# Square sums with a fifth group on GpSimd, rows added before their column sums, and a first fold in quarters

## The chip, the core and the metric

The kernel runs on one core of one Trainium2 chip. The metric is the device time of one execution in microseconds (us), taken as the median of several runs. TensorE does the matrix products (PE in the rows below, PEld for its weight loads), VectorE is DVE, ScalarE is ACT, GpSimd is POOL, and SyncE (SP) issues nearly all DMAs. SBUF is the on-chip memory, PSUM the memory into which TensorE adds up.

## What is computed

Attention over channels, then two feed-forward layers, all in float32 from outside. Cut to what matters:

```python
qn = q / (np.linalg.norm(q, axis=1, keepdims=True) + 1e-06)    # q, k, v: 6016 x 256
kn = k / (np.linalg.norm(k, axis=1, keepdims=True) + 1e-06)
s = kn.transpose(0, 2, 1) @ qn / tau                           # 256 x 256
s = s - s.max(-1, keepdims=True)
a = np.exp(s)
a /= a.sum(-1, keepdims=True) + 1e-09
x = v @ a
h = x @ moe_w_in;  x = (h * np.cos(h)) @ moe_w_out             # 2048 hidden
h = x @ moe2_w_in; x = (h / (1 + np.exp(-h))) @ moe2_w_out
```

The change touches the norms (sums of squares over all 6016 tokens), the softmax, and the place where the softmax is multiplied into the first layer's weights.

## The kernel before

**Loading and scores.** q and k come in 25 groups, two chunks of 128 tokens each but for three groups of one. For each group SP issues a load (L529) into one of seven buffers, TensorE multiplies k by q (L619, two halves of k, `a` = 0 and 1, into `S[0]` and `S[1]`), and ScalarE squares the group (L651). The squares are added up on VectorE into `acc` (L668), except for the groups in `SIDE`, which GpSimd adds into `aside` (L663); one square buffer (`SQ_BUFS`) serves GpSimd's groups, two PSUM buffers serve VectorE's. At group `JOINED` the two sums are added (L670). In the groups named in `FINE` TensorE uses split operands (L608).

**Held-back scores.** For the last `LATE` groups only half `a` = 0 is multiplied in the loop. The other half is kept back as filler for TensorE: some of it behind the column sums, the rest behind the matmul that spreads the norms.

**Norm chain.** TensorE sums `acc` over its 128 partitions with eight one-column products (L677: two rows of 512, four columns blocks each), then one for tau (L678). Then: square root on ScalarE (L683), plus 1e-6 and reciprocal on VectorE (L684, L685), a diagonal matrix `aside` with the norms (L686 on ScalarE, L687 on VectorE), tau (L690, L691), a matmul that spreads the diagonal over all rows (L693), a copy (L696).

**Softmax and fold.** For each half `a`: scaling (L701), maximum (L704), exponential (L705), two transposes on TensorE (L712), a copy to `ET` (L713). The first fold multiplies `ET` into the first 512 columns of the first layer's weights (L761), in halves of 256 columns; ScalarE and VectorE scale the result to a high part (L769) and a low part (L773) in `wa`. Layer one begins after it (L856). The remaining folds (`f1` to `f3`, L743) follow between units of layer one.

**Weights.** The weights come as 64-bit words: a load (`l` for the output weights, `lW` for the input weights, L279), then `a..`/`b..`/`d..` begin with the absolute value on ScalarE (L345) and a rounding of the low word (L297 on ScalarE, L299 on GpSimd), `c..` clamp and shift on VectorE (L304, L312), `j..` join on VectorE and GpSimd (L318, L321), `s..` split on ScalarE and GpSimd (L369, L370). The last letter is W for input and O for output weights. `s0`, `v0`, `s1`, `v1` split the first two blocks of v on ScalarE (L504) and GpSimd (L507).

**Order.** The schedule is written by hand: each engine runs its instructions in the order in which the program emits them, and strings such as `FRONT`, `AFTER`, `BEFORE` and `EARLY` say at which point a step is emitted. A unit `i` of layer one is: products h (L856), sine on ScalarE (L1215), product with the cosine on VectorE (L1218), high part (L867, ScalarE) and low part (L871, VectorE) of the unit before, and the output products of the unit two before (L884).

Of the kernel before, what the change touches and what calls it, by code (L numbers as in the profile page):

```python
# [20 lines left out]
P = 128  # L21
C = 256
# [24 lines left out]
ASIDE = [("wo2", 5), ("wo2", 6), ("wo2", 7)]  # L47
GROUPS = [1, 1] + 22 * [2] + [1]
FIRST = 2
LATE = 4  # L50
REST = 2
TAU = 9
SQ_BUFS = 1
FINE = {5: 'v', 8: 'v', 10: 'v', 13: 'a'}
BEHIND = 3
WARM = (9, 0)
# [11 lines left out]
EARLY = {  # L68
# [3 lines left out]
    'outer': {  # L72
        0: 'x1 l', 1: 'aO', 2: 'p1 cO lW', 3: 'e1 l10 l11 p2 w10 w11', 4: 'l', 5: 'dO', 6: 'rO cO',
        7: 'e2 l20 l21 w20 w21', 9: 'aO', 10: 'cO', 11: 'e3 l30 l31 w30 w31',
    },
}
# [151 lines left out]
def direct(ctx, tc, qk, vT, tau, w_in1, w_out1, w_in2, w_out2, outT, dp, kept, within):  # L228
# [302 lines left out]
    for eng in (nc.sync, nc.scalar, nc.sync):  # L531
# [66 lines left out]

    fine = {}

    def emit_scores(g, both=range(CH)):
        c0 = sum(GROUPS[:g])
        if g in fine:
            kinds = fine[g]
            for j in range(GROUPS[g]):
                for a in both:
                    for i, k in PASSES:
                        nc.tensor.matmul(  # L608
                            S[a],
                            kinds[i][:, j, 1, a * P : (a + 1) * P],  # L610
                            kinds[k][:, j, 0, :],
                            start=False,
                            stop=False,
                            skip_group_check=True,
                        )
            return
        for j in range(GROUPS[g]):
            for a in both:
                nc.tensor.matmul(  # L619
                    S[a],  # L620
                    tiles[g][:, j, 1, a * P : (a + 1) * P],
                    tiles[g][:, j, 0, :],
                    start=(c0 + j == 0),
                    stop=(c0 + j == NCK - 1),
                    skip_group_check=True,
                )

    for g, n in enumerate(GROUPS):
        c0 = sum(GROUPS[:g])
        if g == len(tiles):  # L630
            load_group(nc.sync)
        t = tiles[g]
        if g == 0:
            nc.vector.memset(ones, 1.0)
            nc.vector.memset(rtau, 0.0)
            nc.vector.memset(sums, 1e-9)
            make_identity(nc, ident)
            warm_up(N[:, :P], WARM[0])
# [12 lines left out]
        nc.scalar.activation(sq[:, :n], t[:, :n].rearrange("p g s d -> p g (s d)"), AF.Square)  # L651
        if g in FINE:
            k = len(fine)
            hi, lo = [w[k // 2][:, k % 2].rearrange("p j (s c) -> p j s c", s=2) for w in (wa, wo1)]
            fine[g] = (hi, lo)
            if FINE[g] == "a":
                nc.scalar.activation(hi, t, AF.Copy)
            else:
                nc.vector.tensor_scalar(out=hi, in0=t, scalar1=1.0, scalar2=1.0, op0=ALU.mult, op1=ALU.mult)
            nc.gpsimd.tensor_tensor(out=lo, in0=t, in1=hi.bitcast(F32), op=ALU.subtract)  # L660
        if g in SIDE:
            if g > SIDE[0]:
                nc.gpsimd.tensor_tensor(out=aside, in0=aside, in1=sq, op=ALU.add)  # L663
        elif c0 < GMAX:
            assert c0 + n <= GMAX
            nc.vector.tensor_copy(acc[:, c0 : c0 + n], sq[:, :n])
        else:
            nc.vector.tensor_tensor(out=acc[:, :n], in0=acc[:, :n], in1=sq[:, :n], op=ALU.add)  # L668
        if g == JOINED:
            nc.vector.tensor_tensor(out=acc, in0=acc, in1=aside, op=ALU.add)  # L670
        steps_of(FRONT.get(g, ""))
    steps_of(AFTER)

    for j in range(GMAX - 1, -1, -1):
# [3 lines left out]
    nc.tensor.matmul(N[:, 2 * CH : 2 * CH + 1], ones, rtau, start=False, stop=True, skip_group_check=True)  # L678
    steps_of(THEN[0])
    late = range(len(GROUPS) - LATE, len(GROUPS))  # L680
    for g in late[:REST]:
        emit_scores(g, (1,))
    nc.scalar.activation(r.rearrange("p s a -> p (s a)"), N[:, : 2 * CH], AF.Sqrt)  # L683
    nc.vector.tensor_scalar_add(r, r, 1e-6)  # L684
# [71 lines left out]
    def fold_half(m):  # L756
        fold_room(0, m)
        for a in range(CH):
            pws[0, a] = pws[0, a][:, : TB // 2]
            for d in range(CH):  # L760
                nc.tensor.matmul(  # L761
                    pws[0, a],
                    ET[:, d, a * P : (a + 1) * P],
                    w1[:, d, m * TB // 2 : (m + 1) * TB // 2],
                    start=(d == 0),
                    stop=(d == CH - 1),
                )
        for a in range(CH):
            nc.scalar.activation(fold_to(0, a, 0)[:, m], pws[0, a], AF.Copy, scale=rs[:, a : a + 1])  # L769
# [455 lines left out]
    for i, u in enumerate(units):  # L1225
# [503 lines left out]
```

## Time and profile before

| | |
|---|---|
| median of 3 runs | 991.25 us (990.12 to 991.81) |
| the profiled execution | 991.51 us, of which the span from the first to the last instruction is 989.6 us |
| TensorE busy | 981.4 us, 99% |
| VectorE, ScalarE, GpSimd busy | 822.0, 785.1, 403.6 us |
| granted TensorE clock, mean | 0.999 |

How to read it: a row of a timeline gives start, duration, engine, line, operation, out<-in, shape, count, and in brackets the idle time before it with what ended it. Matmuls are pipelined: one of 256 columns lasts 0.38 us in the record, but the next starts 0.216 us later, and a float32 product is two such instructions.

### The profile page before, as it was taken

The page shows a single profiled execution, that of the slowest core. Times are in us where ns is not written, and L with a number is a line of the kernel's source. Part 1 is how long each engine was busy: PE and PEld are TensorE (multiplying, and loading weights), DVE is VectorE, ACT ScalarE, POOL GpSimd, SP SyncE. Part 2 cuts the span into 40 slices and gives each one's busy share as a digit, 9 for nine tenths or more (in the row PEclk, how much of TensorE's full clock was granted, in tenths as well). Part 3 has the DMA queues.
Part 4 walks back from the last instruction along what each step waited for, and adds up shares of the span by engine and source line. Part 5 has one row for each costly group of instructions (what it writes and reads, how often), then busy time and mean ns, then how long its engine had stood idle before and what let it go on. Part 6 is the DMA issues. An engine that isn't in the chain of part 4 may idle for free.

```text
span 989.6 us, 18765 instructions
## 1 busy us (share of the span) xinstructions
PE 981.4 (99%) x7092; PEld 931.1 (94%) x7092; DVE 822.0 (83%) x1290; ACT 785.1 (79%) x1443; POOL 403.6 (41%) x379
## 2 busy tenths in 40 slices
PE   9999999999999999999999999999999999999997
PEld 8877888899999999999999999999999999999997
DVE  6788779878788878788865899999999999999972
ACT  6786657688888888888876887888888888888863
POOL 4443369657768678677463111111111111111100
PEclk9999999999999999999999999999999999999999
DMA  9931025623433434333579722022022022021001
GB/s 357 379 104 64 1 91 234 250 87 138 138 139 129 160 123 166 128 139 134 207 281 387 289 76 96 13 86 97 12 86 96 13 86 86 24 86 51 31 12 40
DMA packets 35012, 126.59 MB, mean 128 GB/s; under 512 B 3170, under 2 KB 4450, under 8 KB 30178
## 3 DMA queue, kind: packets, MB, share of 16 engines
q1 hardware_dynamic: 34626, 124.86, 34.0%
q8 instruction: 57, 0.93, 0.4%
q10 hardware_dynamic: 288, 0.46, 0.1%
q14 instruction: 41, 0.34, 0.1%
HBM read 73.01 MB, written 52.30 MB: 127 GB/s over the span
## 4 chain that ended last, share of the span: by engine, by line
PE 96%; issue 2%; DVE 1%; POOL 1%; ACT 0%; POOLq 0%
PE xz L1099 21%; PE o L1099 20%; PE o L1466 17%; PE ys L1099 15%; PE o L884 7%; PE h L856 4%; PE S L619 3%; PE o L1139 2%; PE bound L856 1%; PE pw L743 1%; PE xz L1128 1%; PE ys L1128 1%; PE ys L1421 1%; PE xz L1421 1%; PE S L608 1%
## 5 line engine op out<-in xcount | busy, mean ns | idle before, releaser
L915 DVE TENSOR_TENSOR lo<-t,hi 128x768 fp32r<-128x768 f32 (+1 forms) x176 | 194.6, 1115 | 29.2 <-ACT hi L907 29.1
L902 POOL TENSOR_TENSOR t<-t 128x256 f32<-128x256 f32 x88 | 64.4, 731 | 356.9 <-DVE t L899 312.9
L907 ACT ACTIVATE hi<-t 128x768 fp32r<-128x768 f32 (+1 forms) x176 | 169.2, 961 | 27.0 <-PE o L1099 26.3
L1466 PE MATMUL o<-hi,wo 128*128 128x512 f32 x512 | 142.0, 380 | 0.0
L1099 PE MATMUL o<-hi,wo 128*128 128x256 f32 x770 | 134.7, 275 | 0.0
L1099 PEld LDWEIGHTS o<-hi,wo 128*128 128x128 f32 x770 | 117.1, 192 | 0.0
L1099 PE MATMUL o<-lo,wo 128*128 128x256 f32 x385 | 105.9, 275 | 0.0
L1466 PEld LDWEIGHTS o<-hi,wo 128*128 128x128 f32 x512 | 87.4, 190 | 6.8
L1520 DVE TENSOR_TENSOR xz<-xz,t 128x512 f32<-128x512 f32 x64 | 44.7, 699 | 42.1 <-ACT t L1514 41.3
L1466 PE MATMUL o<-lo,wo 128*128 128x512 f32 x256 | 76.1, 380 | 0.0
L1099 PEld LDWEIGHTS ys<-xhi,wf 128*128 128x128 f32 x384 | 67.7, 190 | 6.8
L1099 PE MATMUL ys<-xhi,wf 128*128 128x256 f32 x384 | 74.1, 275 | 0.0
L1099 PEld LDWEIGHTS o<-lo,wo 128*128 128x128 f32 x385 | 73.9, 192 | 0.0
L1099 PE MATMUL xz<-xhi,wa 128*128 128x256 f32 x384 | 71.8, 276 | 0.0
L1625 ACT ACTIVATE ys<-xz 128x256 f32<-128x256 f32 x88 | 32.4, 368 | 45.6 <-PE xz L1099 44.7
L1099 PEld LDWEIGHTS xz<-xhi,wa 128*128 128x128 f32 x384 | 62.8, 191 | 3.4
L1099 PE MATMUL xz<-x2hi,wf 128*128 128x256 f32 x352 | 65.8, 275 | 0.0
L1099 PE MATMUL xz<-x2hi,wa 128*128 128x256 f32 x352 | 65.8, 275 | 0.0
L884 PE MATMUL o<-hi,wo 128*128 128x512 f32 (+1 forms) x256 | 60.7, 373 | 0.5 <-POOL wo L370 0.5
L894 DVE TENSOR_TENSOR t<-t 128x512 f32<-128x512 f32 x88 | 60.3, 686 | 0.1
L1655 ACT ACTIVATE t<-t 128x512 f32<-128x512 f32 x88 | 55.6, 632 | 2.2 <-DVE t L1149 2.1
L1511 ACT ACTIVATE ys<-xz 128x256 f32<-128x256 f32 x64 | 23.6, 368 | 40.6 <-PE xz L1099 39.4
(287 smaller groups left out, 3159.1 us busy)
## 6 DMA issues: line engine op xcount, KB each, us to landing
qk<-qk_dram SPq DMA_DIRECT2D x22, 512.0 KB, 6.1
x2hi<-xshi SPq DMA_DIRECT2D x11, 896.0 KB, 5.0
x2lo<-xslo SPq DMA_DIRECT2D x11, 896.0 KB, 7.3
wi_dram<-stage SPq DMA_DIRECT2D x8, 1024.0 KB, 3.8
wo_dram<-stage SPq DMA_DIRECT2D x8, 1024.0 KB, 4.6
outT_dram<-q SPq DMA_DIRECT2D x22, 256.0 KB, 2.0
vraw<-vT_dram SPq DMA_DIRECT2D x10, 512.0 KB, 4.2
xshi<-t SPq DMA_DIRECT2D x10, 512.0 KB, 5.2
```

Source lines behind the costliest of these rows:

```text
L619: nc.tensor.matmul(S[a], tiles[g][:, j, 1, a * P : (a + 1) * P], tiles[g][:, j, 0, :], start=(c0 + j == 0), stop=(c0 + j == NCK - 1), skip ...
L856: nc.tensor.matmul(hp[:, s, :n], wa_at(i, a, 2 * m + s), columns(x[k][:, a, :n]), start=((i, k) == passes[0] and a == 0), stop=((i, k) == ...
L884: nc.tensor.matmul(o[:, e, :n], wo1_at(i, f)[:, e * P : (e + 1) * P], columns(parts[k][:, s, :n]), start=(f == 0 and (i, k) == PASSES[0]), ...
L894: eng.tensor_tensor(out=t[:, 4:6, :c], in0=t[:, 0:1, :c].to_broadcast([P, 2, c]), in1=t[:, 1:3, :c], op=ALU.subtract)
L902: eng.tensor_tensor(out=t[:, 7, :c], in0=t[:, 3, :c], in1=t[:, 6, :c], op=ALU.subtract)
L907: nc.scalar.activation(hi[:, sl, :c], t[:, 1:][:, sl, :c], AF.Copy)
L915: nc.vector.tensor_tensor(out=lo[:, sl, :c], in0=t[:, 1:][:, sl, :c], in1=hi[:, sl, :c].bitcast(F32), op=ALU.subtract)
L1099: nc.tensor.matmul(out, w(p, ka), columns(x[r][:, kb - 1]), start=(start and i == 0), stop=(stop and i == 2), skip_group_check=True,)
L1466: nc.tensor.matmul(o[:, e], wo1_at(i, f)[:, e * P : (e + 1) * P], columns(parts[k][:, s]), start=(f == 0 and (i, k) == PASSES[0]), stop=(f ...
L1520: nc.vector.tensor_tensor(out=xz[k], in0=xz[k], in1=sines[:, 1], op=ALU.mult)
L1625: nc.scalar.activation(y2, x2, AF.Copy)
L1655: nc.scalar.activation(t[:, 0:2], t[:, 0:2], AF.Silu)
```

## The change

The fifth group for GpSimd: `SIDE` is 7, 11, 15, 18, 21 in place of 7, 11, 15, 20. The two sums are joined after the last group, and the two rows of `acc` are then added on VectorE, so that the column sums need four products in place of eight; tau's product stands ahead of them. `LATE` is 5 in place of 4, and three chunks stand behind the column sums, six behind the spreading matmul (four and three before). The first load of output weights (`l`) moves from behind all groups to between groups 22 and 23; the join of the first input weights (`jW`) moves from group 17 to 18. The split of v's first block (`s0 v0`) moves to ahead of the column sums. The square root goes to PSUM, and two tensor-scalar products become scalar-tensor-tensor ones. The softmax is emitted half by half, with a begin of input weights and the join of output weights (`jO`) between; the first fold goes in quarters (`q00 q10 q01 q11`), the second half's transposes between. In layer one the join `jW` of unit 5 moves behind the cosine product, and the low part of unit 5 (`p5`) moves behind unit 6's cosine product.

```diff
-LATE = 4
-REST = 2
+LATE = 5
+REST = 3
-FRONT = {14: 'lW aW', 15: 'cW', 17: 'jW'}
-AFTER = 'l V lv lW aO l lW cO'
-THEN = ['', '', 'jO s0', '']
-SIDE = [7, 11, 15, 20]
-JOINED = 22
-BEFORE = 'v0 s1 v1 T0 T1 bW rs f00 x0 l00 w00 f01 l01 w01 tb'
+FRONT = {14: 'lW aW', 15: 'cW', 18: 'jW', 22: 'l'}
+AFTER = 'V lv lW aO l lW s0 v0 cO'
+SIDE = [7, 11, 15, 18, 21]
+BEFORE = 's1 v1 lw q00 T1 q10 rs q01 h0 q11 x0 l00 w00 h1 l01 w01 tb'
-    'inner': {4: 'aW cW', 5: 'sO jW', 8: 'aW cW', 9: 'sO jW', 13: 'sO'},
+    'inner': {4: 'aW cW', 5: 'sO', 8: 'aW cW', 9: 'sO jW', 13: 'sO'},
-... 4: 'l', 5: 'dO', 6: 'rO cO',
+... 4: 'l', 5: 'jW dO', 6: 'p5 rO cO',
...
-        if g == JOINED:
-            nc.vector.tensor_tensor(out=acc, in0=acc, in1=aside, op=ALU.add)
         steps_of(FRONT.get(g, ""))
+    nc.vector.tensor_tensor(out=acc, in0=acc, in1=aside, op=ALU.add)
+    nc.vector.tensor_tensor(out=acc[:, 0], in0=acc[:, 0], in1=acc[:, 1], op=ALU.add)
     steps_of(AFTER)
-    for j in range(GMAX - 1, -1, -1):
-        for i in range(2 * CH):
-            nc.tensor.matmul(N[:, i : i + 1], acc[:, j, i * P : (i + 1) * P], ones[:, 0:1], **st)
-    nc.tensor.matmul(N[:, 2 * CH : 2 * CH + 1], ones, rtau, ...)
+    nc.tensor.matmul(N[:, 2 * CH : 2 * CH + 1], ones, rtau, start=True, **small_sum)
+    for i in range(2 * CH):
+        nc.tensor.matmul(N[:, i : i + 1], acc[:, 0, i * P : (i + 1) * P], ones[:, 0:1], start=False, **small_sum)
...
-    nc.vector.tensor_scalar_mul(aside[:, 0, P:C], ident, r[:, 0, 1:2])
+    nc.vector.scalar_tensor_tensor(
+        out=aside[:, 0, P:C], in0=ident, scalar=r[:, 0, 1:2], in1=ident, op0=ALU.mult, op1=ALU.mult
+    )
-    nc.vector.tensor_scalar_mul(r[:, 1], r[:, 1], rtau)
+    nc.vector.scalar_tensor_tensor(
+        out=r[:, 1], in0=r[:, 1], scalar=rtau, in1=ones[:, :CH], op0=ALU.mult, op1=ALU.mult
+    )
...
+    scaled(0)
+    maxima(0)
+    exponential(0)
+    begin_w1()
+    steps_of("jO")
+    scaled(1)
+    emit_turn(0)
+    maxima(1)
+    exponential(1)
...
-            if i != 3:
+            if i not in (3, 6):
                 emit_low(pend)
```

## Rows read from the trace of the kernel before

**Rows 1.** Page, part 1: busy time, share of the span and instructions
```profile
PE 981.4 (99%) x7092; PEld 931.1 (94%) x7092; DVE 822.0 (83%) x1290; ACT 785.1 (79%) x1443; POOL 403.6 (41%) x379
```

**Rows 2.** Waits of PE: total us, times, longest
```profile
PE pt L712 <- ACT E L705: 1.3, 2, 0.9
```

**Rows 3.** Timeline of PE, 41 to 54.5 us
```profile
42.53 1.84 PE L677 MATMUL S<-ones,acc 128*128 128x1 f32 x16
...
46.70 1.46 PE L619 MATMUL S<-qk 128*128 128x256 f32 x6
...
53.40 0.78 PE L856 MATMUL h<-xhi,wa 128*128 128x512 f32 x2
```

**Rows 4.** DMA issues at 17.85, 29.68, 31.40, 37.23, 37.73 us: KB, us to landing
```profile
qk<-qk_dram SPq DMA_DIRECT2D x1, 512.0 KB, 9.6
...
qk<-qk_dram SPq DMA_DIRECT2D x1, 512.0 KB, 6.4
...
qk<-qk_dram SPq DMA_DIRECT2D x1, 512.0 KB, 5.9
...
raw_w<-w_in_dram SPq DMA_DIRECT2D x1, 1024.0 KB, 9.6
...
raw_wo<-w_out_dram SPq DMA_DIRECT2D x1, 1024.0 KB, 12.1
```

**Rows 5.** Timeline of DVE, 32 to 51 us
```profile
39.25 1.23 DVE L670 TENSOR_TENSOR acc<-acc,aside 128x1024 f32<-128x1024 f32 x1
40.58 2.01 DVE L668 TENSOR_TENSOR acc<-acc,sq 128x1024 f32<-128x1024 f32 x2
...
45.79 1.22 DVE L318 SCALAR_TENSOR_TENSOR wv_wo<-raw_wo,wv_wo 128x1024 int32<-128x1024 int32 x1
46.93 0.42 DVE L696 COPY rq<-S 128x256 f32<-128x256 f32 x1
...
47.90 0.42 DVE L704 TENSOR_REDUCE nmax<-E 128x1 f32<-128x256 f32 x1
```

**Rows 6.** Timeline of ACT, 37 to 49 us
```profile
37.85 1.03 ACT L651 ACTIVATE sq<-qk 128x1024 f32<-128x1024 f32 x1 [0.30 <-DVE acc L668]
...
42.25 1.14 ACT L297 ACTIVATE raw_wo<-raw_wo 128x1024 int32<-128x1024 uint32 x1
44.63 0.17 ACT L683 ACTIVATE r<-S 128x4 f32<-128x4 f32 x1 [1.24 <-PE S L678]
45.34 0.40 ACT L686 ACTIVATE aside<-ident,r 128x128 f32<-128x128 f32 x1 [0.53 <-DVE r L685]
...
48.77 0.19 ACT L705 ACTIVATION_READ_ACCUMULATOR E<-E,nmax 128x1 f32 x1
```

**Rows 7.** Timelines of DVE, then POOL, 82 to 93 us
```profile
83.97 1.50 DVE L318 SCALAR_TENSOR_TENSOR w<-raw_w,w 128x1024 int32<-128x1024 int32 x1
...
87.78 3.38 DVE L871 TENSOR_TENSOR lo<-t,hi 128x1024 fp32r<-128x1024 f32 x1 [1.18 <-ACT hi L867]
...
84.13 3.57 POOL L370 TENSOR_TENSOR wo<-wv_wo,wo 128x1024 fp32r<-128x1024 f32 x1 [1.17 <-ACT wo L369]
87.67 2.41 POOL L321 TENSOR_TENSOR w<-w,raw_w 128x1024 int32<-128x1024 int32 x1
```

**Rows 8.** Timeline of PE, 85 to 96 us
```profile
87.76 1.13 PE L884 MATMUL o<-hi,wo 128*128 128x512 f32 x4 [0.47 <-POOL wo L370]
...
91.75 0.59 PE L856 MATMUL h<-xlo,wa 128*128 128x512 f32 x2
92.44 3.67 PE L743 MATMUL pw<-w,ET 128*128 128x512 f32 x8
```

**Rows 9.** Clock: busy us by stretch, PEclk near the end; PE at the start
```profile
984.00:987.00 3.00, 0.60 (x4) 0.31 (x2) 0.00 (x0) 0.65 (x2) 0.00 (x0) 0.97 0.41 142
987.00:989.60 2.60, 0.00 (x0) 0.00 (x0) 0.00 (x0) 0.00 (x0) 0.00 (x0) 0.50 0.05 13
...
5.09 1.91 PE L619 MATMUL S<-qk 128*128 128x256 f32 x4
```

More of the change, by code (lines that the diff above doesn't have):

```diff
@@ L55 @@
 BEHIND = 3
-WARM = (9, 0)
-FRONT = {14: 'lW aW', 15: 'cW', 17: 'jW'}
-AFTER = 'l V lv lW aO l lW cO'
-THEN = ['', '', 'jO s0', '']
-SIDE = [7, 11, 15, 20]
-JOINED = 22
-BEFORE = 'v0 s1 v1 T0 T1 bW rs f00 x0 l00 w00 f01 l01 w01 tb'
+WARM = 9
+FRONT = {14: 'lW aW', 15: 'cW', 18: 'jW', 22: 'l'}
+AFTER = 'V lv lW aO l lW s0 v0 cO'
+SIDE = [7, 11, 15, 18, 21]
+BEFORE = 's1 v1 lw q00 T1 q10 rs q01 h0 q11 x0 l00 w00 h1 l01 w01 tb'
 TURNS = 16
@@ L69 @@
     'amid': {0: 'cW', 2: 'hW', 3: 'f1', 7: 'f2', 11: 'f3'},
[1 row of a table removed]
[1 row of a table added]
     'mid': {0: 'sO', 4: 'jO', 8: 'jO', 12: 'jO'},
     'outer': {
-        0: 'x1 l', 1: 'aO', 2: 'p1 cO lW', 3: 'e1 l10 l11 p2 w10 w11', 4: 'l', 5: 'dO', 6: 'rO cO',
+        0: 'x1 l', 1: 'aO', 2: 'p1 cO lW', 3: 'e1 l10 l11 p2 w10 w11', 4: 'l', 5: 'jW dO', 6: 'p5 rO cO',
         7: 'e2 l20 l21 w20 w21', 9: 'aO', 10: 'cO', 11: 'e3 l30 l31 w30 w31',
@@ L588, in direct @@
         "p2": lambda: emit_low(2),
+        "p5": lambda: emit_low(5),
     }
@@ L599, in direct, with emit_scores @@
     fine = {}
-    def emit_scores(g, both=range(CH)):
+    def emit_scores(g, both=range(CH), chunks=range(GMAX)):
         c0 = sum(GROUPS[:g])
@@ L616, in emit_scores @@
             return
-        for j in range(GROUPS[g]):
+        for j in chunks[: GROUPS[g]]:
             for a in both:
@@ L637, in direct @@
             make_identity(nc, ident)
-            warm_up(N[:, :P], WARM[0])
+            warm_up(N[:, :P], WARM)
         if g == TAU:
@@ L668, in direct @@
             nc.vector.tensor_tensor(out=acc[:, :n], in0=acc[:, :n], in1=sq[:, :n], op=ALU.add)
-        if g == JOINED:
-            nc.vector.tensor_tensor(out=acc, in0=acc, in1=aside, op=ALU.add)
         steps_of(FRONT.get(g, ""))
+    nc.vector.tensor_tensor(out=acc, in0=acc, in1=aside, op=ALU.add)
+    nc.vector.tensor_tensor(out=acc[:, 0], in0=acc[:, 0], in1=acc[:, 1], op=ALU.add)
     steps_of(AFTER)
-    for j in range(GMAX - 1, -1, -1):
-        for i in range(2 * CH):
-            st = dict(start=(j == GMAX - 1 and i == 0), stop=(j == 0), skip_group_check=True)
-            nc.tensor.matmul(N[:, i : i + 1], acc[:, j, i * P : (i + 1) * P], ones[:, 0:1], **st)
@@ L678, in direct @@
[L678 to L684, printed above, removed]
+    small_sum = dict(stop=True, skip_group_check=True)
+    nc.tensor.matmul(N[:, 2 * CH : 2 * CH + 1], ones, rtau, start=True, **small_sum)
@@ L685, in direct @@
+    for i in range(2 * CH):
+        nc.tensor.matmul(N[:, i : i + 1], acc[:, 0, i * P : (i + 1) * P], ones[:, 0:1], start=False, **small_sum)
+    late = [(g, j) for g in range(len(GROUPS) - LATE, len(GROUPS)) for j in range(GROUPS[g])]
+    for g, j in late[:REST]:
+        emit_scores(g, (1,), (j,))
+    roots = N[:, 4 * CH : 6 * CH]
+    nc.scalar.activation(roots, N[:, : 2 * CH], AF.Sqrt)
+    nc.vector.tensor_scalar_add(r.rearrange("p s a -> p (s a)"), roots, 1e-6)
     nc.vector.reciprocal(r, r)
@@ L693, in direct, with begin_w1, scaled @@
     nc.tensor.matmul(N[:, C:], ones, aside[:, 0, :C], start=True, stop=True)
-    for g in late[REST:]:
-        emit_scores(g, (1,))
+    for g, j in late[REST:]:
+        emit_scores(g, (1,), (j,))
     nc.vector.tensor_copy(rq, N[:, C:])
-    steps_of(THEN[3])
-    for a in range(CH):
+    def begin_w1():
+        W1.begin(low=False)
+    calls["lw"] = lambda: W1.round_low(W1.begun[0][1])
+    def scaled(a):
         nc.vector.scalar_tensor_tensor(
@@ L703, in direct, with maxima, exponential @@
         )
+    def maxima(a):
         nc.vector.tensor_reduce(out=nmax[:, a : a + 1], in_=E[:, a], axis=AX.X, op=ALU.max, negate=True)
-        nc.scalar.activation(
-            E[:, a], E[:, a], AF.Exp, bias=nmax[:, a : a + 1], accum_out=sums[:, a, 0:1]
-        )
+    def exponential(a):
+        nc.scalar.activation(E[:, a], E[:, a], AF.Exp, bias=nmax[:, a : a + 1], accum_out=sums[:, a, 0:1])
     pts = [ps_hs[a].tile([P, 2, TB], F32, tag="h", name=f"pt{a}") for a in range(CH)]
@@ L724, in inverse_sums @@
         nc.vector.reciprocal(rs, rs)
-    calls.update(T0=lambda: emit_turn(0), T1=lambda: emit_turn(1), tb=table, rs=inverse_sums)
+    calls.update(T1=lambda: emit_turn(1), tb=table, rs=inverse_sums)
     turn_of = [0]
@@ L754, in fold_high, with fold_quarter, fold_high_half @@
         )
-    def fold_half(m):
-        fold_room(0, m)
-        for a in range(CH):
[L759 to L769, printed above, removed]
+    pw_halves = {}
+    def fold_quarter(m, a):
+        if a == 0:
+            fold_room(0, m)
+            pw_halves[m] = [pws[0, i][:, : TB // 2] for i in range(CH)]
+        for d in range(CH):
+            nc.tensor.matmul(
+                pw_halves[m][a],
+                ET[:, d, a * P : (a + 1) * P],
+                w1[:, d, m * TB // 2 : (m + 1) * TB // 2],
+                start=(d == 0),
+                stop=(d == CH - 1),
+            )
+    def fold_high_half(m):
+        for a in range(CH):
+            nc.scalar.activation(fold_to(0, a, 0)[:, m], pw_halves[m][a], AF.Copy, scale=rs[:, a : a + 1])
     def fold_low_half(m):
@@ L774, in fold_low_half @@
                 out=fold_to(0, a, 1)[:, m],
-                in0=pws[0, a],
+                in0=pw_halves[m][a],
                 scalar=rs[:, a : a + 1],
@@ L808, in direct @@
         for a in range(CH):
-            calls[f"f0{a}"] = lambda a=a: fold_half(a)
+            calls[f"h{a}"] = lambda a=a: fold_high_half(a)
+            for m in range(2):
+                calls[f"q{m}{a}"] = lambda m=m, a=a: fold_quarter(m, a)
             calls[f"l{j}{a}"] = (lambda j=j, a=a: fold_low(j, a)) if j else (lambda a=a: fold_low_half(a))
```

3 lines of the change are left out of this document (removed).

## The prediction

> **What bounds the kernel now.** The page's busy shares come first: TensorE is busy for 981.4 of 989.6 us [rows 1], so whatever the change does reaches the end only through TensorE's idle time or its work. The waits of TensorE say where that idle time is: 1.3 us before the transposes of the softmax [rows 2], and 0.47 us for split weights at 87.3 us [rows 8]. From 42.53, where the column sums begin, to 53.40, where layer one begins, TensorE has no other gap [rows 3]. So the best case is small: 1.3 + 0.47 us of waits, the four column sums that go (eight of sixteen instructions, 0.106 us apart: 0.85 us [rows 3]), and some 0.3 us at 92 us, together 2.9 us or 0.3%. What can be lost has no such limit: TensorE now walks into the column sums without waiting, and everything behind it counts. The question is therefore when `acc` is ready; I read that from DMA landings, ScalarE, VectorE and GpSimd, in this order.
>
> **Part 1, TensorE reaches the sums earlier.** With group 20's second half held back, two products (four instructions, 0.216 us apart by the six in 1.46 us [rows 3]) move behind the sums: TensorE is there at 42.53 - 0.86 = 41.67, and at 41.9 after tau's product.
>
> **Part 2, the moved load makes the last groups late.** SP's loads land in the order of issue and the DMAs are busy throughout: group 22, issued at 29.68, lands 6.4 later at 36.1, group 23, issued at 31.40, at 37.3, so 1.2 us for 512 KB [rows 4]. The load `l` of 1 MB is now issued at about 30.1, between the two. Such a load of output weights landed at 37.73 + 12.1 = 49.8, 3.0 us behind the load before it (37.23 + 9.6 = 46.8) [rows 4]. The bounds are twice a group's 1.2, 2.4 us, and 3.0 us; I take 3.0, the same kind of load. That a load ahead holds up a group is seen at 17.85: that group was issued behind 1 MB of weights and took 9.6 us [rows 4]. So group 23 lands at 36.1 + 3.0 + 1.2 = 40.3 in place of 37.3. SP itself does not wait there, and the first block of v lands no later than before, since the bytes ahead of it are the same. TensorE needs group 23 at 40.4 (41.67 less six instructions), just in time. ScalarE's square, which began at 37.85 [rows 6], can't.
>
> **Part 3, `acc` is ready at 45.6.** From landing: square 1.03 with 0.08 of signalling [rows 6]; the adds of groups 23 and 24, 2.01; the join, 1.23; the new add of two rows, 0.69 (the 512-column add in the 2.01: 2.01 - 1.22 - 0.10); 0.1 between dependent adds, twice [rows 5]. Together 5.24, so F = 40.3 + 5.24, about 45.6. The fifth group on GpSimd takes 1.2 us off VectorE, but VectorE is not what is late any more. GpSimd's queue (group 18, then the moved join `jW`, then group 21, 2.4 us each [rows 7]) is through at about 41.0, before the join needs it. TensorE waits from 41.9 to 45.6: **3.7 us**.
>
> **Part 4, from the sums to layer one.** Written from F. Four sums: to F+0.95. Square root to diagonal took 44.63 to 45.74 [rows 6]: diagonal at F+2.2, while three chunks (1.30) fill TensorE to F+2.25: no wait. The spreading matmul (0.43) and six chunks (2.59) take it to F+5.3. Copy, scaling and maximum of the first half (46.93 to 48.32 [rows 5]) end at F+4.3, the exponential (to 48.96, 0.64 [rows 6]) at F+4.95: hidden under the six chunks, so the first transpose no longer waits. Next late is the copy of that transpose: it stands on VectorE behind `jO` (1.22 [rows 5], F+4.2 to F+5.4) and the second scaling, which needs the last chunk (F+5.5 to F+6.0), and ends at F+6.3. TensorE, free at F+5.6, waits 0.75. Then a quarter fold (0.86), 0.14 for the second exponential, transposes, three quarters: layer one at F+10.3. Idle in all 3.7 + 0.75 + 0.14 = 4.6, against 1.3; with 0.85 less work the stretch is longer by 4.6 - 1.3 - 0.85 = **+2.45 us**. Layer one at 45.6 + 10.3 = 55.9 against 53.40 [rows 3] gives +2.5, the same. Free by cover: `begin_w1` (F+5 to F+6.1, before the second exponential at F+6.7), `s1` behind that, `v1` and `lw` on GpSimd (as far into layer one as before).
>
> **Part 5, GpSimd against VectorE.** `v0` now runs ahead of the sums. ScalarE does group 24's square, two steps of the output weights and `s0`, each of the three 1.14 [rows 6], from 41.9: `v0` comes at 45.2. The rows show that GpSimd and a VectorE instruction with two SBUF inputs exclude each other: the split at 84.13 took 3.57 in place of 2.4, since the join from 83.97 to 85.47 ran, and the low part at 87.78 took 3.38, since GpSimd was busy until 90.08 [rows 7]. So `v0` waits for the new add and runs from 45.6 to about 47.9, and VectorE's half of the diagonal, now a product with two SBUF inputs, wants to run at F+1.75 = 47.3: about **+0.4 us**. The clamp and shift `cO` (one SBUF input) stand on VectorE between F and F+1.4, ahead of the norm chain at F+1.3. No row shows such an instruction beside GpSimd; its price lies between 0 and the wait for `v0`, 2.3. I take 0, since the exclusion is shown for two inputs only; the upper end is a rival.
>
> **Part 6, the clock.** The granted clock fell to 0.50, 1.2 GHz, within 2.4 us of TensorE's last matmul (0.60 us after 984 [rows 9]); the waits of before, 0.9 at most [rows 2], left it at 2.4 GHz. A wait of 3.7 us is longer than the one that let it fall. At 1.2 GHz instructions of 256 columns are 0.43 us apart (four in 1.91 [rows 9]) in place of 0.216, and after the launch TensorE still ran so from 5.09 to 7.0 us. Half of a stretch of 7.0, 3.5, is the upper end, 0 the lower; part of a slow stretch falls into waits, so I take somewhat less than the middle, **+1.5 us**.
>
> **Part 7, layer one.** With `jW` behind the cosine product, the split at 84.13 finds GpSimd free, ends at 86.5 and TensorE's 0.47 us is gone [rows 7, 8]. With the low part of unit 5 behind unit 6's cosine product, that product no longer waits out the 3.38; it is what frees the buffer of fold `f2`, which began at 92.44 where TensorE could have begun at 91.75 + 0.43 = 92.18 [rows 8]: 0.26. Together **-0.7 us**. Covers: the joined weights are there at 90.3, fold `f2` wants them at 91.5; the low part ends near 91.4, its first reader comes after `f2`, past 94.5.
>
> **Sum.** 2.5 + 0.4 + 1.5 - 0.7 = +3.7 us. The profiled execution was 991.51 (989.6 of span and 1.9 around it), 0.3 above the median; on the median's scale, 991.25 + 3.7 = **995.0 us**.
>
> **The rivals.** (a) The clock stays up: 991.25 + 2.5 + 0.4 - 0.7 = 993.4, give or take 0.6 for the load's price. For it: the mean clock is 0.999 with gaps of 1.3 us; against: the fall at the end. (b) `cO` waits for `v0`: the clamp starts at 47.9, the norm chain 2.3 us late in place of 0.4, so 995.4, and up to 996.9 with what the clock adds. The Trainium skill, "SBUF — State Buffer", section "Who interferes with whom", says that a VectorE `tensor_scalar` in its mode with two ports takes the pair shared with GpSimd for the whole instruction, as an instruction with two SBUF inputs does; by that rule (b) holds. No row here has both at once. (c) Not slower: the moved load doesn't hold group 23. It decides at a landing of 38.2: then F is 43.4, TensorE waits 1.5, and the whole comes to nothing. If landings stay as they are and VectorE runs through, F is 40.58 + 2.01 [rows 5] less an add of 1.3 and with the new one of 0.8, 42.1; it is up to 1.7 later, 43.8, where ScalarE's squares wait for GpSimd's single square buffer (by the exclusion of part 5, `jW` on VectorE holds group 18's add for up to 1.2 us). By part 4 that is -1.0 to +0.7, with 0 to 0.4 of part 5 and -0.7 of part 7, so 989.5 to 991.7. For it: TensorE itself is barely touched by the load; against: the 9.6 us of the earlier case [rows 4].
>
> **How the numbers follow.** Forecast (late `acc`, clock falls) 0.40; (a) 0.15; (b) 0.15; (c) 0.30. A measurement of this kernel tells about 0.2%, 2 us, from no change: 989.3 to 993.2. Forecast, (b) and half of (a) are slower by more than that, 0.62; half of (a) and 0.20 of (c) are the same, 0.28; 0.10 of (c), where the waits of part 4 shrink as well, is faster. The range reaches from 989.4 to 997.0 and leaves out the ends of (c) and (b).
>
> **What would show it.** TensorE's first tau product near 41.7 and a wait of some 3.7 us before the sums; group 23's load landing about 9 us after its issue; its square near 40.3; a granted clock below 1 around 45 to 52 us; `v0` across the diagonal's product; no wait before the first transpose but one before the first quarter; no wait for split weights near 87 us. If the landing stays below 38, parts 2, 3 and 6 fall together. If the wait is there but the clock is flat, only part 6 falls.

## The result and the profile after

The changed kernel takes **996.37 us** (median of 6 runs, 995.85 to 996.51); the kernel before, run beside it, 991.17 (6 runs, 990.12 to 992.13). The ratio is 1.0051, 95% interval 1.0041 to 1.0062: slower, by 5.2 us. The forecast was 995.0, with a range of 989.4 to 997.0. The profiled execution has a span of 994.4 us (989.6 before) and a mean granted clock of 0.996 (0.999).

Busy shares have hardly moved [rows 1]: TensorE is still at 99%, so the loss is in waits and in the clock. Page of after, part 1 (busy time, share, instructions):

```profile
PE 983.3 (99%) x7084; PEld 931.9 (94%) x7084; DVE 823.5 (83%) x1290; ACT 785.0 (79%) x1443; POOL 404.3 (41%) x380
```

Waits of TensorE in after (us in total, times, longest). The wait for the softmax [rows 2] is gone; one for the column sums has come, and one for the quarters of the fold (0.69 us, in the next timeline):

```profile
PE S L676 <- DVE acc L670: 2.9, 1, 2.9
```

Timeline of TensorE in after, 41 to 58 us (start, duration, engine, line, operation, out<-in, shape, count, idle time before). L674 is tau's product, L676 the column sums, L876 layer one (L856 before). Compare [rows 3]: the six instructions behind the sums took 1.46 us there in the like case and take 2.91 here.

```profile
41.08 0.28 PE L674 MATMUL S<-rtau,ones 128*128 128x1 f32 x2
44.30 1.87 PE L676 MATMUL S<-ones,acc 128*128 128x1 f32 x8 [2.94 <-DVE acc L670]
46.02 2.91 PE L618 MATMUL S<-qk 128*128 128x256 f32 x6
48.72 1.14 PE L693 MATMUL S<-aside,ones 128*128 128x256 f32 x2
...
52.61 0.38 PE L718 MATMUL pt<-ident,E 128*128 128x128 f32 x2
53.68 1.13 PE L777 MATMUL pw<-w,ET 128*128 128x256 f32 x4 [0.69 <-DVE ET L719]
...
57.38 0.85 PE L876 MATMUL h<-xhi,wa 128*128 128x512 f32 x2
```

The clock over the same stretch: the third column from the right is the granted clock (1.00 is 2.4 GHz, 0.50 is 1.2 GHz). Read in finer stretches it falls at 43.56, while TensorE waits, and is back at 50.39.

```profile
41.00:44.00 3.00, 0.35 (x4) 0.24 (x2) 2.76 (x4) 2.75 (x3) 0.18 (x1) 0.93 0.98 358
44.00:47.00 3.00, 2.71 (x10) 2.54 (x11) 3.00 (x2) 0.16 (x1) 2.50 (x1) 0.50 1.02 395
47.00:50.00 3.00, 3.00 (x8) 2.19 (x7) 1.74 (x8) 1.82 (x3) 0.00 (x0) 0.50 0.68 267
50.00:53.00 3.00, 2.99 (x14) 2.33 (x12) 2.55 (x5) 1.72 (x4) 0.49 (x1) 0.94 0.02 7
```

Why `acc` is late: timelines of VectorE, ScalarE and GpSimd in after. The square of group 23 waits for its DMA (L650); the join (L669) and the row addition (L670) stand behind the last group's addition. Then the clamp (L302, 0.69 us in before: the last row here) takes 2.89 and ends 0.6 behind `v0` (L505), which is through at 46.5; the diagonal's product (L685) comes 1.6 us after `v0`.

```profile
40.17 2.01 DVE L667 TENSOR_TENSOR acc<-acc,sq 128x1024 f32<-128x1024 f32 x2 [2.38 <-ACT sq L650]
42.29 1.23 DVE L669 TENSOR_TENSOR acc<-acc,aside 128x1024 f32<-128x1024 f32 x1
43.55 0.69 DVE L670 TENSOR_TENSOR acc<-acc 128x512 f32<-128x512 f32 x1
44.16 2.89 DVE L302 TENSOR_SCALAR wv_wo<-wv_wo 128x1024 f32<-128x1024 f32 x1
...
48.09 0.35 DVE L685 SCALAR_TENSOR_TENSOR aside<-ident,r 128x128 f32<-128x128 f32 x1
...
39.11 1.54 ACT L650 ACTIVATE sq<-qk 128x1024 f32<-128x1024 f32 x2 [2.57 <-DMA qk<-qk_dram]
...
43.82 2.67 POOL L505 TENSOR_TENSOR xlo<-v,xhi 128x1024 fp32r<-128x1024 f32 x1 [4.62 <-ACT xhi L502]
...
42.51 0.69 DVE L304 TENSOR_SCALAR wv_wo<-wv_wo 128x1024 f32<-128x1024 f32 x1
```

DMA issues of after at 29.47 and 29.09 us (KB, us to landing): the moved load lands at 37.7, 3.15 behind group 22, which lands at 34.6. Group 23, issued at 30.81, comes behind it.

```profile
raw_wo<-w_out_dram SPq DMA_DIRECT2D x1, 1024.0 KB, 8.2
qk<-qk_dram SPq DMA_DIRECT2D x1, 512.0 KB, 5.5
```

Layer one, timelines of TensorE and GpSimd in after: the split L368 takes 2.41 us in place of 3.57 [rows 7], and fold `f2` (L757) follows the products without a gap [rows 8].

```profile
95.34 0.59 PE L876 MATMUL h<-xlo,wa 128*128 128x512 f32 x2
95.78 3.60 PE L757 MATMUL pw<-w,ET 128*128 128x512 f32 x8
...
88.45 2.41 POOL L368 TENSOR_TENSOR wo<-wv_wo,wo 128x1024 fp32r<-128x1024 f32 x1 [1.17 <-ACT wo L367]
```

**Where the 5 us come from.** Take the same matmul in both traces and subtract its start in before from its start in after; the difference is called the shift. The first 20 us of an execution already differ by 0.0 to 1.5 us from one to the next, so each shift below is taken less that of its own first 20 us (-0.59 in after). After is +4.98 at 60 us, +3.85 at 100 us and +4.74 from 560 us on; with the start and 0.6 more behind the last matmuls that is the 4.8 between the spans.

### The profile page after: what moved, and what is told of

Its sections match the earlier page's. It is cut to its first block, busy times and chain, and to the rows that moved or that the text cites. A ratio compares the mean times of both kernels' runs of the same rounds, so it can differ in the third digit from the quotient of the medians.

```text
span 994.4 us, 18747 instructions
## 1 busy us (share of the span) xinstructions
PE 983.3 (99%) x7084; PEld 931.9 (94%) x7084; DVE 823.5 (83%) x1290; ACT 785.0 (79%) x1443; POOL 404.3 (41%) x380
## 4 chain that ended last, share of the span: by engine, by line
PE 95%; ACT 2%; DVE 1%; DMA 1%; issue 0%; ACTq 0%; DVEq 0%; SPq 0%
PE o L1119 20%; PE xz L1119 20%; PE o L1486 16%; PE ys L1119 15%; PE o L904 8%; PE h L876 4%; PE S L618 3%; PE o L1159 2%; PE bound L876 1%; PE pw L757 1%; DMA qk<-qk_dram 1%; PE xz L1148 1%; PE ys L1148 1%; PE xz L1441 1%; PE ys L1441 1%
```

## The experiments

All times are medians, each ratio against runs of before taken beside them on the same chip; the chips differ between rows, and before took 991.0 to 991.4 on them. The shifts are those of TensorE in the profiled execution, less its start.

| kernel | us | ratio (95%) | shift at 60 | at 100 | at 600 |
|---|---|---|---|---|---|
| changed kernel | 996.37 | 1.0051 (1.0041 to 1.0062) | +4.98 | +3.85 | +4.74 |
| e1: load back | 993.13 | 1.0029 (1.0016 to 1.0042) | +2.86 | +1.78 | +2.63 |
| e2: v0 back | 995.44 | 1.0039 (1.0023 to 1.0054) | +5.16 | +4.08 | +4.87 |
| e3: both back | 992.07 | 1.0012 (1.0003 to 1.0022) | +0.67 | -0.41 | +0.37 |
| e4: before with the layer-one part | 989.97 | 0.9985 (0.9976 to 0.9994) | -0.01 | -1.09 | -1.07 |
| e5_warm: wait filled | 996.45 | 1.0056 (1.0041 to 1.0072) | +6.46 | +5.38 | +6.27 |
| e5_warm_v0_back: wait filled, v0 back | 993.02 | 1.0020 (1.0010 to 1.0029) | +2.29 | +1.21 | +2.12 |
| e7: e4 with LATE = 5 | 989.63 | 0.9988 (0.9979 to 0.9997) | +0.46 | -0.62 | -0.14 |
| e9: before with LATE = 5 | 991.50 | 1.0004 (0.9995 to 1.0013) | +0.02 | +0.03 | +0.06 |
| e10: before, load moved | 991.02 | 1.0003 (0.9994 to 1.0013) | +0.01 | +0.01 | +0.03 |
| e11: before, v0 moved | 993.14 | 1.0019 (1.0009 to 1.0029) | +1.91 | +1.95 | +2.45 |
| e12: e11 with the new norm chain | 991.95 | 1.0016 (1.0006 to 1.0025) | +2.66 | +2.66 | +2.69 |
| e13: changed, old sums, load and v0 back | 990.85 | 0.9999 (0.9990 to 1.0008) | -0.05 | -1.13 | -0.38 |

### The load and v0 taken back, one by one and together

```diff
 # e1 (and e3)
-FRONT = {14: 'lW aW', 15: 'cW', 18: 'jW', 22: 'l'}
-AFTER = 'V lv lW aO l lW s0 v0 cO'
+FRONT = {14: 'lW aW', 15: 'cW', 18: 'jW'}
+AFTER = 'l V lv lW aO l lW s0 v0 cO'
 # e2 (and e3)
-AFTER = '... s0 v0 cO'
-BEFORE = 's1 v1 ...'
+AFTER = '... s0 cO'
+BEFORE = 'v0 s1 v1 ...'
```

> The changed kernel, with the first load of output weights issued behind all groups again, as before the change; all else stays. Theory (the load holds group 23 by 3 us, and the late sums bring the wait of the clamp and the slow clock with them): group 23 lands some 3 us earlier, the added rows are ready about 2.3 us earlier, TensorE waits under 1 us before the sums, the clamp runs before v0 starts on GpSimd, the granted clock stays at 1, and the time is 990.5 to 991.5 us, 5 to 6 below the changed kernel's 996.4. Rival (GpSimd's fifth group with its single square buffer makes the sums late): the wait before the sums stays at 2 us or more and the time at 995.5 to 996.5.

> The changed kernel, with GpSimd's split of v's first block (v0) emitted behind the softmax again; its ScalarE half stays ahead of the sums and the load stays early. Theory (the clamp on VectorE waits for v0, 2.2 us, and the norm chain stands behind the clamp): the clamp takes 0.7 in place of 2.9 us, TensorE's wait before the sums stays at 2.9 us, the half clock stays, and the time is 994.2 to 995.0, some 1.4 to 2.2 below 996.4, since the slow clock then takes a part of what the clamp gives back. Rival (the wait of the clamp lies beside TensorE's work at half clock and costs nothing): 996.0 to 996.5.

> The changed kernel with both undone: load behind all groups, v0 behind the softmax. Theory (the wait for v0 costs only because the sums are late): within 0.5 us of the run with the load alone moved back, 990.5 to 991.5. Rival (the two costs stand by themselves and add up): 1.5 to 2 us below that run.

Measured: 993.13, 995.44 and 992.07. The load is worth 3.2 us by the medians and 2.1 by the shifts, less than the theory's 5 or 6. The five executions of e1 are of two sorts: three have a mean clock of 0.999 or 1.0 and take 992.5 to 993.1 us (the profiled one is among them), two have 0.996 and 0.997 and take 995.5 and 995.8. So the slow stretch seems to come here too in some executions; no trace of these two was kept. What is left in e1 shows in VectorE's timeline: the bit shift (L310, 0.69 us when free) now meets `v0`, and TensorE waits for the diagonal (waits of e1, below it).

```profile
42.90 2.78 DVE L310 TENSOR_SCALAR wv_wo<-wv_wo 128x1024 int32<-128x1024 int32 x1
...
PE S L693 <- ACT aside L684: 1.8, 1, 1.8
PE S L676 <- DVE acc L670: 1.8, 1, 1.8
```

In e2 the clamp takes its 0.69 us, and yet in the profiled execution layer one begins no earlier (+5.16): VectorE's timeline, the clock, then TensorE's. TensorE at half clock is the later of the two, so by this trace the rival was right: the clamp's wait lies beside slow work. By the times it is undecided: the median lies between both forecasts, two of the four executions took 996.1 and 996.2 (the latter was profiled), two 994.4 and 994.8.

```profile
44.56 0.69 DVE L302 TENSOR_SCALAR wv_wo<-wv_wo 128x1024 f32<-128x1024 f32 x1
...
44.00:47.00 3.00, 2.30 (x10) 2.21 (x11) 2.12 (x5) 0.32 (x2) 0.00 (x0) 0.51 1.03 393
...
57.79 0.85 PE L876 MATMUL h<-xhi,wa 128*128 128x512 f32 x2
```

With the load back as well (e3), the same `v0` is worth 2.2 us of shift (2.86 to 0.67) and 1.1 of the medians, so the theory that it costs only where the sums are late fails. "No cost" in e2 is cover, not absence. In e3 a wait of 1.6 us for `acc` remains. By the timelines it comes through the single square buffer: GpSimd's addition of group 18 is held up by the join on VectorE (3.22 in place of 2.4 us, so 0.8 of the 1.6), ScalarE waits for it, VectorE for ScalarE. No run takes this apart. Timelines of e3, VectorE, GpSimd, ScalarE, TensorE:

```profile
31.08 1.22 DVE L316 SCALAR_TENSOR_TENSOR w<-raw_w,w 128x1024 int32<-128x1024 int32 x1
...
36.56 3.34 DVE L667 TENSOR_TENSOR acc<-acc,sq 128x1024 f32<-128x1024 f32 x3 [1.81 <-ACT sq L650]
...
31.30 3.22 POOL L662 TENSOR_TENSOR aside<-aside,sq 128x1024 f32<-128x1024 f32 x1 [1.18 <-ACT sq L650]
...
34.56 2.92 ACT L650 ACTIVATE sq<-qk 128x1024 f32<-128x1024 f32 x3 [1.47 <-POOL aside L662]
...
42.01 1.05 PE L676 MATMUL S<-ones,acc 128*128 128x1 f32 x8 [1.58 <-DVE acc L670]
```

The ten runs of e3 are not alike: six have a mean clock of 0.999 or 1.0 and take 990.7 to 992.2 us, four have 0.996 to 0.998 and take 992.8 to 994.7. In these four the wait of 1.6 us has probably let the clock fall; the profiled run is of the first sort, so that is argued, not shown.

### The layer-one part alone

```diff
-    'inner': {..., 5: 'sO jW', ...},
+    'inner': {..., 5: 'sO', ...},
-    'outer': {..., 5: 'dO', 6: 'rO cO', ...},
+    'outer': {..., 5: 'jW dO', 6: 'p5 rO cO', ...},
-            if i != 3:
+            if i not in (3, 6):
```

> The kernel before with the change in layer one alone: the join behind unit 5's cosine product, and the low part of unit 5 behind unit 6's. Theory: TensorE's 0.47 us wait for split weights goes, with the slow restart after it (0.74 in all), and the third fold begins 0.34 us earlier against the products ahead of it: 990.1, that is 0.9 to 1.2 below 991.2. Rival (what is gained there is waited out at the next late step): 991.0 to 991.3.

Measured 989.97. The shift is 0 up to 87 us, -0.75 from 88 us on, -1.09 from 93 us on, and stays to the end: the part is worth 1.1 us by the trace and 1.3 by the medians, and the changed kernel has the same step between 60 and 100 us.

### The wait filled, so that the clock stays up

```diff
 # e5_warm; e5_warm_v0_back has the edit of e2 as well
+    warm_up(N[:, C : C + P], 12)
     small_sum = dict(stop=True, skip_group_check=True)
     nc.tensor.matmul(N[:, 2 * CH : 2 * CH + 1], ones, rtau, start=True, **small_sum)
```

> The changed kernel with 12 products of ones by ones put between tau's product and the column sums, into columns that are written over later. They fill the wait of 2.94 us, so that TensorE has no long gap there; all else is as in the changed kernel. Theory (the clamp's wait for v0 and the fall of the clock lie over each other): the granted clock stays at 1.0 up to the column sums; the clamp still takes 2.9 us, so TensorE, now fast, waits some 2 us ahead of the spreading matmul, and layer one begins only about 0.8 us earlier: 995.6 us. Rival (the halved clock alone sets the stretch): 6.8 us at half clock are worth 3 us, 993.3. Third way: the clock falls in the new wait instead, and nothing is won, 996.4.

> The changed kernel with the same 12 products in the wait and with v0 moved back to behind the norm chain: neither the halved clock nor the clamp's wait is left, only the late group 23 is. Theory (each of the two hides the other, and both gone give 2.9 us): layer one at about 54.9 us in place of 57.8 us, so 995.44 - 2.9 = 992.5 to 993.4. Rival (the halved clock costs nothing on the path, since TensorE would only wait for VectorE): as with v0 moved back alone, 995.4.

Measured: 996.45 and 993.02. The products stand ahead of tau's product, not behind it as expected; of the wait 0.78 us are left. In e5_warm the third way came true. Its TensorE timeline and clock: no fall from 41 to 47 us, but now TensorE waits 1.92 us for the norm chain, behind the clamp, and the clock falls at 49.92, 0.8 us after that wait.

```profile
49.13 0.67 PE L694 MATMUL S<-aside,ones 128*128 128x256 f32 x2 [1.92 <-ACT aside L685]
49.64 4.44 PE L618 MATMUL S<-qk 128*128 128x256 f32 x12
...
41.00:44.00 3.00, 2.97 (x27) 2.87 (x25) 2.76 (x3) 3.00 (x4) 0.00 (x0) 1.00 1.04 413
44.00:47.00 3.00, 2.25 (x14) 1.95 (x14) 2.99 (x2) 0.45 (x2) 2.59 (x1) 1.00 1.02 387
...
50.00:54.00 4.00, 4.00 (x13) 3.16 (x12) 2.30 (x4) 2.17 (x5) 1.55 (x1) 0.58 0.00 0
```

With both gone, layer one starts at 54.10 (57.79 in e2; on the scale of before 55.3 and 58.2) and the clock is 1.00 in every stretch from 38 to 60 us. Timeline of TensorE and clock in e5_warm_v0_back:

```profile
46.74 2.75 PE L618 MATMUL S<-qk 128*128 128x256 f32 x12
...
54.10 0.85 PE L877 MATMUL h<-xhi,wa 128*128 128x512 f32 x2
...
44.00:47.00 3.00, 3.00 (x18) 2.64 (x19) 2.26 (x8) 1.42 (x3) 0.00 (x0) 1.00 1.05 403
```

This is the price of the clock: e2 and e5_warm_v0_back differ in nothing but the filler, their sums begin at the same time (45.1 us on the scale of before in both), and the shift at 60 us is 5.16 against 2.29, **2.9 us**. The medians differ by 2.4 us, the ratios by 0.0019 (1.9 us), and the means of the two sorts of executions of e1 by 2.8: so 2 to 3 us, 2.9 in the traces. The length of the stretch agrees: 6.83 us at half clock in after, of which 0.74 lie in the wait, and half of the other 6.09 is 3.0.

### The load and v0 moved alone, in the old order

```diff
 # e10
-FRONT = {14: 'lW aW', 15: 'cW', 17: 'jW'}
-AFTER = 'l V lv lW aO l lW cO'
+FRONT = {14: 'lW aW', 15: 'cW', 17: 'jW', 22: 'l'}
+AFTER = 'V lv lW aO l lW cO'
 # e11 (and e12)
-AFTER = 'l V lv lW aO l lW cO'
-THEN = ['', '', 'jO s0', '']
-BEFORE = 'v0 s1 v1 ...'
+AFTER = 'l V lv lW aO l lW s0 v0 cO'
+THEN = ['', '', 'jO', '']
+BEFORE = 's1 v1 ...'
 # e12 as well: square root into PSUM, both tensor-scalar products as in the changed kernel
```

> The kernel before with the load of output weights moved to between groups 22 and 23, and nothing else. Theory (the late landing costs only because the join and the row addition now stand behind the last group's addition): in the old order VectorE does the join from 39.25 us and comes to group 23 at 40.58 us, and group 23's square, begun at 39.1 us as in the changed kernel, is done by then; acc is ready at 42.6 us as before, and the time is that of the kernel before, 991.0 (within 0.5). Rival (the landing alone makes acc late, whatever the order): by the 3.2 us between the changed kernel and that with the load moved back, 993 to 994.2.

> The kernel before with the split of v's first block (s0 v0) moved to ahead of the clamp of output weights, and nothing else. ScalarE is through with s0 at about 44.5 us, so v0 takes GpSimd from 44.5 to 46.9 us, when the clamp and the shift are over and VectorE's norm chain (one SBUF input each) is to run. Theory (a tensor-scalar instruction waits for GpSimd's whole instruction, whatever its size): the chain starts at 46.9 in place of 44.84 us, the spreading matmul 2.1 us late, 993.1. Rival (only the large instructions wait, the four and 128 columns of the chain do not; the join behind it, with two SBUF inputs, waits to 46.9 us): the first maximum 1.1 us late, 992.1. Third: nothing waits, 991.0.

> The same with the norm chain as in the changed kernel: square root into PSUM, and both products as scalar-tensor-tensor instructions. Theory of the prediction (a product with two SBUF inputs waits for v0, a sum read from PSUM does not): the chain begins at 44.8 us, the diagonal's product ends at 47.2 in place of 45.5 us, and the spreading matmul comes 1.2 us late; the join waits in any case: 992.3 to 992.8. Rival (this form does not wait): only the join does, 992.1, and the diagonal's product shows its 0.35 us while v0 runs.

Measured: 991.02, 993.14 and 991.95. **e10**: the late landing alone costs nothing. Group 23's square waits for its DMA as in the changed kernel, but VectorE does the join in the meantime, and its additions end at 41.43, while TensorE sums the first row, without a wait. Timelines of ScalarE, VectorE and TensorE:

```profile
38.35 1.55 ACT L651 ACTIVATE sq<-qk 128x1024 f32<-128x1024 f32 x2 [2.56 <-DMA qk<-qk_dram]
...
37.48 1.23 DVE L670 TENSOR_TENSOR acc<-acc,aside 128x1024 f32<-128x1024 f32 x1
39.41 2.02 DVE L668 TENSOR_TENSOR acc<-acc,sq 128x1024 f32<-128x1024 f32 x2 [0.70 <-ACT sq L651]
...
41.00 1.84 PE L677 MATMUL S<-ones,acc 128*128 128x1 f32 x16
```

**e11**: the theory's time, and its reason: an instruction of four columns waits for the whole of `v0` (0.17 us in before: the last row). VectorE, then GpSimd:

```profile
44.57 2.11 DVE L684 TENSOR_SCALAR r<-r 128x4 f32<-128x4 f32 x1 [1.01 <-ACT r L683]
...
44.26 2.40 POOL L507 TENSOR_TENSOR xlo<-v,xhi 128x1024 fp32r<-128x1024 f32 x1 [6.52 <-ACT xhi L504]
...
44.84 0.17 DVE L684 TENSOR_SCALAR r<-r 128x4 f32<-128x4 f32 x1 [0.92 <-ACT r L683]
```

**e12**: the same sum read from PSUM and the reciprocal run beside `v0`; the product with two SBUF inputs waits till it is through at 46.3 (1.34 in place of 0.35 us).

```profile
44.70 0.16 DVE L685 TENSOR_SCALAR r<-S 128x4 f32<-128x4 f32 x1 [0.96 <-ACT S L684]
44.90 0.18 DVE L686 RECIPROCAL r<-r 128x4 f32<-128x4 f32 x1
45.12 1.34 DVE L688 SCALAR_TENSOR_TENSOR aside<-ident,r 128x128 f32<-128x128 f32 x1
...
43.91 2.40 POOL L507 TENSOR_TENSOR xlo<-v,xhi 128x1024 fp32r<-128x1024 f32 x1 [5.24 <-ACT xhi L504]
```

So the theory's wait is there, though the median is 0.35 below the theory's range and 0.15 below the rival's 992.1. The shift is +1.03 ahead of the fold; in the profiled execution it grows to +2.66 at 60 us, since the clock is at 0.56 from 51 to 54 us, behind waits of 0.4 and 1.3 us. That execution took 994.0; six of the ten took 991.7 to 992.0, four 993.5 to 994.2, and only two of these four show a lower mean clock (0.997). The ten of e11 spread likewise, 991.7 to 994.8, with no lower clock in any. Before spreads by 2.2 by itself; what makes the rest is open.

### More held-back products, and the change without its new sums

```diff
 # e7: before with the edit of e4; the label e9_load_alone is a slip: it has this one line and moves no load
-LATE = 4
+LATE = 5
 # e13: the changed kernel with FRONT (17: 'jW', no 22), AFTER = 'l V lv lW aO l lW s0 cO', BEFORE = 'v0 s1 ...' and
-SIDE = [7, 11, 15, 18, 21]
+SIDE = [7, 11, 15, 20]
+        if g == 22: # the join here, not behind the last group; no addition of rows; eight sums, then tau
```

> The kernel before with the two moves in layer one and with LATE = 5 alone, so that two more products stand behind the spreading matmul. Theory: they fill the waits ahead of the softmax's transposes, while the column sums begin 0.86 us earlier and wait about 0.4 us for the last half of acc: 0.3 to 0.85 us under the layer-one part alone, 989.2 to 989.7. Rival: acc is what is late, and the earlier arrival of TensorE turns into a wait of 0.86 us: 990.0.

> The kernel before with LATE = 5 alone, without the moves in layer one. Theory (the two parts do not touch each other): 1.3 us above the kernel with both, so 990.5 to 991.0. Rival: the gain in layer one depends on the phase in which it is entered, and the difference is not 1.3.

> The changed kernel with the order of the square sums taken back to that of the kernel before (four groups on GpSimd, the join behind group 22, no addition of the rows, eight column sums, tau last), and with the load and v0 taken back as well. What is left of the change: held-back products in chunks of three and six, the norm chain's forms, the softmax half by half, the fold in quarters, the moves in layer one. Theory (all of the loss is in the square sums' order, with what the load and v0 add to it; the rest is a gain): no wait before the column sums, layer one 7.8 us behind the spreading matmul with six chunks between, 7.4 for the five chunks of the kernel with LATE = 5 and the moves in layer one, which took 8.0; so 0.6 below that kernel's 989.6, 989.0 us, and 3 us below the changed kernel with both taken back (992.1). Rival (the fold in quarters gains nothing, its 0.69 us of waiting replaces the wait for the softmax): 989.6 to 990.0. Second rival (the loss lies in the softmax and fold part): 992.

Measured: 989.63, 991.50 and 990.85. LATE = 5 by itself is worth nothing (shift +0.02, interval across 1), and e7 can't be told from e4 by their intervals: my theory that the products fill the waits for the softmax fails, since one wait of 1.24 us for the second half's exponential takes the place of the two of 0.85 and 0.41. e7 and e9 are one program up to unit 5 of layer one, past 80 us, yet their shifts at 60 us are +0.46 and +0.02: the shift of a single execution is good to about half a microsecond. e13 was to give 989.0 and gave 990.85. Its sums and its fold do what was expected (no wait for `acc`, layer one 7.83 us behind the spreading matmul), and its shift at 60 us is 0.5 below that of e7, no more than single executions differ; 0.8 of that and of layer one's gain is lost again by 600 us (0.46 of it at the place near 472 us described below). Its median is above e7's, though the intervals of the ratios overlap and the two profiled spans are alike (988.0 and 988.1). Whether it is slower than e7, and why, is open. What e13 does say: without the new sums, the load and `v0`, the change costs nothing that can be measured. Of the kernels run, e7 and e4 are the fastest, faster than before by 0.1%.

## Why the prediction was right, point by point

**Direction and range held; the time was 1.4 us too low.** By steps:

- Part 1 (TensorE earlier): tau's product at 41.08, on the scale of before 41.67, as said.
- Part 2 (landing): 3.15 us for the load against 3.0. Right as a landing; group 22 ahead of it landed at 35.2 on the scale of before, not 36.1.
- Part 3 (`acc`): ready at 44.24, 44.8 on the scale of before, against 45.6; the wait is 2.94 against 3.7. Group 23 landed 0.7 earlier than said, the chain behind it took what was said.
- Part 4 (to layer one): no wait before the first transpose, 0.69 before the first quarter (0.75 said). Parts 2 to 4 together were put at +2.45. What they cost with the clock up and `v0` back is the shift of e5_warm_v0_back, **+2.29**.
- But its reason was half the truth: the prediction put the loss on the landing. e10 shows that the landing costs nothing while the join and the additions have room for it; e3 shows +0.67 from the new order without it. It takes both: the landing, and an order in which 1.9 us of VectorE's work stand behind the last group.
- Part 5 (GpSimd): `v0` came 0.8 us earlier than said (44.4 for 45.2 on the scale of before), and its cost was put on the diagonal's product. In the changed kernel that is not touched (0.35); the clamp is (2.89). The price of 0 for the clamp was the wrong choice. That is rival (b): a wait of 2.2 us. Why it did not cost 2.2: TensorE at half clock was as late as the chain (e2: -0.18 of shift, 0.9 us of the medians, where the intervals overlap). With the clock up it costs 2.2 (e1 against e3). The rule quoted for (b) from the Trainium skill ("SBUF — State Buffer", "Who interferes with whom") agrees with the trace: 0.69 became 2.89, 2.78 in e1, and 0.17 became 2.11 in e11. The rule that the prediction itself used, for two SBUF inputs, holds too (0.35 became 1.34 in e12).
- Part 6 (clock): it fell, 43.56 to 50.39, as said; its price was **mis-sized**: 1.5 was taken between 0 and 3.5, and it is 2.9 by the traces. The reason given for going below the middle, that a part of the slow stretch falls into waits, holds for 0.74 us of the 6.83 only: the stretch had no wait but the one in which it began.
- Part 7 (layer one): -1.1 against -0.7. The mechanisms are those named; the wait for split weights took 0.74 us with it and not only its own 0.47, the one at `f2` 0.34 for 0.26.
- Not foreseen: +0.9 us between 100 and 560 us, in several places. The kernels built on the changed one lose 0.75 to 0.91 there, e7 and e11 0.5, e4, e9, e10 and e12 nothing. About half has a place, near 472 us: VectorE's split of v there starts behind GpSimd's instruction instead of 0.02 us ahead of it, and takes 1.93 us in place of 1.12. All fourteen traces agree: in the nine where GpSimd starts first, TensorE's shift grows by 0.43 to 0.56 us there; in the five where VectorE does (before, e4, e9, e10, e12) by nothing. Why GpSimd is first, and the rest of the 0.9, stay open. VectorE, then GpSimd, first in before, then in after:

```profile
468.51 1.12 DVE L507 TENSOR_TENSOR xlo<-vraw,xhi 128x768 fp32r<-128x768 f32 x1
...
468.53 3.46 POOL L380 TENSOR_TENSOR stage<-wv_wo,stage 128x512 fp32r<-128x512 f32 x2
...
472.35 1.93 DVE L505 TENSOR_TENSOR xlo<-vraw,xhi 128x768 fp32r<-128x768 f32 x1
...
471.98 3.40 POOL L378 TENSOR_TENSOR stage<-wv_wo,stage 128x512 fp32r<-128x512 f32 x2
```

So the shift at 600 us is 2.3 (landing and order) + 2.9 (clock) - 0.2 (clamp, covered) - 1.1 (layer one) + 0.9 = +4.8, where 2.45 + 1.5 + 0.4 - 0.7 = 3.7 was said. The terms are read off one trace after another, so that they add up is no proof of any of them. That the forecast came this near is partly luck: three terms were put 0.2 to 0.6 us too high, which took off half of what the clock and the unforeseen part were short. The time alone could not tell the forecast from rival (b), whose 995.4 to 996.9 holds the measured 996.37, and whose wait was there; e2 and e1 against e3 tell them apart. Rival (a) falls with the clock; the "gaps of 1.3 us" quoted for it are two waits together, the longest 0.9 [rows 2]. Of rival (c), "the moved load doesn't hold group 23" is refuted, but its side remark, that the single square buffer behind the held addition of group 18 makes `acc` late, is what the timelines of e3 show; the shift of 0.67 lies within the -1.0 to +0.7 given there.

## What to carry to other kernels

A late transfer costs nothing as long as the engine behind it has other work to put in front: before a reduction's last steps are moved to the end, ask which transfer they were covering. A wait of 2 or 3 microseconds on TensorE can cost twice, by itself and by the slow stretch that follows. Two prices can also hide each other, as the wait of VectorE and the slow stretch did here: taking one away then shows nothing, and only the kernel without both shows what either is worth. Where GpSimd and VectorE meet, look at the form of the VectorE instruction and not at its size: four columns waited 1.9 us.

## What the runs showed of the hardware

- The granted clock fell inside a wait of 2.94 us ahead of the column sums (behind tau's product) and stayed at 0.50 for 6.8 us of nearly full work; in e5_warm it held through 2.8 us of products of ones and fell behind a wait of 1.92.
- In e12 it fell behind waits of 0.37 and 1.28 us, in e11 it did not behind waits of 1.30 and 1.22, nor in e1 behind waits of 1.78 and 1.80, by their profiled executions. The length of a single wait does not tell which way it goes.
- VectorE beside a running GpSimd instruction with SBUF operands: a tensor-scalar sum from SBUF to SBUF waits (0.17 became 2.11), the same sum read from PSUM doesn't (0.16), a reciprocal from SBUF to SBUF doesn't (0.18), a scalar-tensor-tensor product with two SBUF inputs does (0.35 became 1.34).
- In after `v0` began at 43.82, during the row addition (43.55 to 44.24); the clamp that follows directly on VectorE did not get in ahead of it.
